# A Fourier mixer whose instructions are issued from one list of steps with a lead each

## Chip, core and metric

The kernel runs on one core of a Trainium2 chip. The metric is the device time in microseconds of one execution; lower is better. The core's engines run side by side: TensorE (PE; PEld are its weight loads), VectorE (DVE), ScalarE (ACT), GpSimd (POOL) and SyncE (SP, which only issues transfers here). Each engine takes its own instructions strictly in the order in which the program issued them.

## What is computed

A Fourier mixer, a dense squared-ReLU layer and a top-1 mixture of eight experts, on 8 sequences of 3072 tokens of width 256 (for the experts' sake the gate's part is left out here):

```python
def _attn_ref(x, w_r, w_i, b_r, b_i):
    X = np.fft.rfft(x, axis=1)
    Yr = Xr @ w_r - Xi @ w_i + b_r
    Yi = Xr @ w_i + Xi @ w_r + b_i
    Yr = np.sign(Yr) * np.maximum(np.abs(Yr) - 0.01, 0.0)
    Yi = np.sign(Yi) * np.maximum(np.abs(Yi) - 0.01, 0.0)
    return np.fft.irfft(Yr + 1j * Yi, n=3072, axis=1)
def _moe_ref(x, w_in, w_out):
    h = np.maximum(x @ w_in, 0.0)
    return (h * h) @ w_out
```

The weights `w_in` and `w_out` come in as 64-bit floats and are converted on the chip. Products are made to full single precision by splitting each operand into a high and a low part (tiles ending in `h` and `l`); `mm3` at L155 to L158 issues the three products high x high, high x low and low x high.

## The kernel before, in words

The Fourier transform of length 3072 is done as 48 x 64. The mixer's function `fft` has three streams of work.

`gen_a` (the x tiles, 64 of them, eight a sequence): load a tile of 96 x 1024 (L310), split it (xh and half of xl on VectorE, L317 and L318, the other half of xl on GpSimd, L319), six products with the constant `cc`, two copies out of PSUM on ScalarE (L336), one store to the DRAM scratch `ad` (L337).

`gen_b` (96 groups: 24 frequencies j for each of four pairs of sequences). Of a group: read bt from `ad`, two groups at a time (L354); load the tables tm (L360 for the first 24, which are also stored to `tmd` at L361, L363 for the others); split bt into bh and bl on VectorE (L375, L376); s2, three products, and the copy xe on ScalarE (L386); s3, four transposes (L393), then th from PSUM on ScalarE (L397), its negated half (L398), tl on VectorE (L399) and tl's negated half on ScalarE (L411); s4, 24 products with the mixing weights; y, the sum with the bias (L434) and t, its clamp (L435), on VectorE; y minus t on GpSimd (L436); the split into zh on ScalarE (L444) and zl on VectorE (L445); s5, three products, the copy gt on ScalarE (L457) and, every second group, the store to `gd` (L461).

`gen_w` converts `w_in` and `w_out` in 16 steps of eleven yields each; seven yields hold a VectorE operation, three a GpSimd operation, two a ScalarE operation.

The order is that of the generators. Before the loop 17 rounds of `gen_a` run, with the loads of the constants after the first, the mixing weights' loads in rounds 8 and 14 and two of `gen_w`'s loads in round 15. Then iteration t of `gen_b` issues, in this order for all engines: s3 of group t+1, s5 of t-2, s2 of t+2, the rest of s3, the reads and the split of t+3; then the x tile that is due (16 in 24 iterations), one yield of `gen_w`, the first half of s4 of t, another yield, zl and zh of t-1, the second half of s4, y, t and y minus t. There are eight PSUM banks in one ring, `ring()`, taken by s2, s3, s4, s5 and twice by an x tile. In the last two iterations the first tile of the next stage is read back (`c_load`, `c_split`) and transformed (`gen_c`).

After `fft`, `moe()` does the dense layer and the experts; the change does not touch it.

Of the kernel before, what the change touches and what calls it, by code (L numbers as in the profile page):

```python
# [122 lines left out]

def _step(gens, n=1):
    for _ in range(n):
        for g in gens:
            next(g, None)
# [8 lines left out]
def kernel(  # L136
# [15 lines left out]
    def f32(ap):  # L152
        return ap.bitcast(F32)
# [61 lines left out]
    def fft():  # L215
        with ExitStack() as es:
# [15 lines left out]

            def load_mix():
                raws = []
                for i, w in enumerate((w_r, w_i)):
                    raw = p2.tile([P, 2, 2, D], F32, tag="bt", name="raw", bufs=3)[:, 0]
                    SP.dma_start(out=raw, in_=w.rearrange("(c p) d -> p c d", p=P))
                    raws.append(raw)
                for v in range(2):
                    SP.dma_start(out=bias[0:64, v], in_=b_r.unsqueeze(0).to_broadcast([64, D]))  # L240
                    SP.dma_start(out=bias[64:128, v], in_=b_i.unsqueeze(0).to_broadcast([64, D]))
                SP.dma_start(out=bias[127:128, 1], in_=b_r.unsqueeze(0))
                yield
# [3 lines left out]
                yield  # L247
# [54 lines left out]
            def gen_a():  # L302
                NA = 8 * B
                xts, sp = {}, {}

                def load(i):
                    b, c = divmod(i, 8)
                    xt = pa2.tile([96, 4, D], F32, tag="xt", name="xt", bufs=3)
                    src = x[b].rearrange("(p t) d -> p (t d)", t=32)
                    SP.dma_start(out=xt.rearrange("p s d -> p (s d)"), in_=src[:, 4 * c * D:(4 * c + 4) * D])  # L310
                    xts[i] = xt

                def split(i):
                    xt = xts.pop(i).rearrange("p s d -> p (s d)")
                    xh = pa2.tile([96, 1024], F32R, tag="xh", name="xh")
                    xl = pa2.tile([96, 1024], F32R, tag="xl", name="xl")
                    V.tensor_copy(xh, xt)  # L317
                    V.tensor_sub(xl[:, :512], xt[:, :512], f32(xh[:, :512]))  # L318
                    G.tensor_sub(xl[:, 512:], xt[:, 512:], f32(xh[:, 512:]))  # L319
                    sp[i] = xh, xl  # L320

                for i in range(2):
                    load(i)
                for i in range(NA + 1):
                    if i + 2 < NA:
                        load(i + 2)
                    if i >= 1:
                        k = i - 1
                        b, c = divmod(k, 8)
                        xh, xl = sp.pop(k)  # L330
                        at = pa2.tile([96, 1024], F32, tag="at", name="at")
                        for q in range(2):
                            ps = ring()[:96]
                            sl = slice(q * 512, q * 512 + 512)
                            mm3(ps, cc[:, 0], cc[:, 1], xh[:, sl], xl[:, sl])
                            A.copy(at[:, sl], ps)  # L336
                        (A if k < 16 else SP).dma_start(  # L337
                            out=ad[b].rearrange("r (h t) d -> (r h) (t d)", h=2)[:, c * 1024:(c + 1) * 1024], in_=at)
                    if i < NA:
                        split(i)  # L340
                    yield

            NG = NJ * NP_

            def gen_b():
                bts, bs, xs, tt, ys, zs, gts, tms = {}, {}, {}, {}, {}, {}, {}, {}
                NJB = 2

                def load(jb):
                    pr, jb_ = divmod(jb, NJ // NJB)  # L350
                    bt = p2.tile([P, 2, NJB, D], F32, tag="bt", name="bt", bufs=3)
                    for bb in range(2):
                        src = ad[2 * pr + bb].rearrange("(j c) s d -> (c s) j d", c=2)
                        SP.dma_start(out=bt[:, bb], in_=src[:, jb_ * NJB:(jb_ + 1) * NJB, :])  # L354
                    bts[jb] = bt

                def load_t(j):
                    tm = p3.tile([P, 4, P], F32R, tag="tm", name="tm", bufs=7)
                    if j < NJ:
                        G.dma_start(out=tm, in_=c_tm[j])  # L360
                        SP.dma_start(out=tmd[j], in_=f32(tm))  # L361
                    else:
                        SP.dma_start(out=f32(tm), in_=tmd[j % NJ])  # L363
                    tms[j] = tm

                def s1(j):
                    jb, jj = divmod(j, NJB)
                    if jj == 0 and jb + 2 < NG // NJB:
                        load(jb + 2)
                    if j + 1 < NG:  # L370
                        load_t(j + 1)
                    src = bts[jb][:, :, jj, :]
                    bh = p2.tile([P, 2, D], F32R, tag="bh", name="bh")
                    bl = p2.tile([P, 2, D], F32R, tag="bl", name="bl")
                    V.tensor_copy(bh, src)  # L375
                    V.tensor_sub(bl, src, f32(bh))  # L376
                    bs[j] = bh, bl

                def s2(j):
                    bh, bl = bs.pop(j)  # L380
                    tm = tms[j]
                    ps = ring()
                    bh, bl = (a.rearrange("p b d -> p (b d)") for a in (bh, bl))
                    mm3(ps, tm[:, 0], tm[:, 1], bh, bl)
                    xe = p2.tile([P, 4, P], F32, tag="xe", name="xe")
                    A.copy(xe.rearrange("p a b -> p (a b)"), ps)  # L386
                    xs[j] = xe

                def s3(j):
                    xe = xs.pop(j)  # L390
                    ps = ring().rearrange("p (a q) -> p a q", a=4)
                    for a in range(4):
                        T.transpose(ps[:, a], xe[:, a], ident)  # L393
                    th = p2.tile([P, 4, 256], F32R, tag="th", name="th")
                    tl = p2.tile([P, 4, 256], F32R, tag="tl", name="tl")
                    if j % NJ:
                        A.copy(th[:, :, 64:192], ps)  # L397
                        A.activation(th[:, :, 0:64], ps[:, :, 64:128], AF.Copy, scale=-1.0)  # L398
                        V.tensor_sub(tl[:, :, 64:192], ps, f32(th[:, :, 64:192]))  # L399
                    else:  # L400
                        A.copy(th[:, :, 0:128], ps)
                        A.activation(th[:, :, 128:192], ps[:, :, 64:128], AF.Copy, scale=-1.0)
                        A.copy(th[:, :, 192:256], ps[:, :, 0:64])
                        V.tensor_sub(tl[:, :, 0:128], ps, f32(th[:, :, 0:128]))
                        V.tensor_copy(tl[:, :, 192:256], f32(tl[:, :, 0:64]))
                    tt[j] = th, tl

                def s3b(j):
                    th, tl = tt[j]
                    if j % NJ:  # L410
                        A.activation(tl[:, :, 0:64], f32(tl[:, :, 128:192]), AF.Copy, scale=-1.0)  # L411
                    else:
                        V.tensor_scalar(out=tl[:, :, 128:192], in0=f32(tl[:, :, 64:128]), scalar1=-1.0, scalar2=None, op0=ALU.mult)
                        for t in (th, tl):
                            for q in (191, 255):
                                V.tensor_scalar(out=t[:, :, q:q + 1], in0=ident[:, 0:4].unsqueeze(2), scalar1=0.0, scalar2=None, op0=ALU.mult)

                def s4(j):
                    th, tl = tt.pop(j)
                    o1, o2 = (64, 0) if j % NJ else (0, 128)  # L420
                    ps = ring()
                    for bb in range(2):
                        n = 0
                        for i, o in ((0, o1), (1, o2)):
                            for dc in range(2):
# [3 lines left out]
                        if bb == 0:  # L429
                            yield 1  # L430
# [584 lines left out]
```

## Time and profile before

| | us |
|---|---|
| median of three runs (4115.95 to 4117.76) | 4116.31 |
| the profiled execution | 4116.9 |
| its span, from first to last instruction | 4115.1 |
| of the span, TensorE busy | 3999.2 (97%) |
| VectorE busy | 3096.0 (75%) |
| ScalarE busy | 1970.1 (48%) |
| GpSimd busy | 987.5 (24%) |

A busy share is a sum over the span; the mixer takes about the first sixth of it, and the engines' shares there are others. TensorE's matmuls overlap, so that its busy time is not its peak. Two operations of VectorE back to back overlap by about 0.1 us: the start of one and the start of the next give its real cost, their durations a little more. An instruction that waits for a resource after it has started shows that wait as duration.

### The profile page before, as it was taken

To read this page: it belongs to the slowest core of one execution; us is meant where nothing else is said; L and a number is where in the kernel's file an instruction comes from. 1 tells how busy PE (TensorE), PEld (TensorE's weight loads), DVE (VectorE), ACT (ScalarE), POOL (GpSimd) and SP (SyncE) were. 2 spreads that over 40 slices of the span, in tenths; PEclk is the share of its full clock that TensorE was granted. 3 is DMA by queue.
4 is the path that set the end of the run, shared out by engine and by line. 5 is a ranking of instruction groups with operands and counts; after the bars stand their busy time and mean duration, and the time that the engine had idled before them with its cause. 6 is when DMAs were issued, how large, how long until landed. Compare 5 with 4: busy or idle time off the path is not lost. (4 is left out here: it accounts for less than half of the span.)

```text
span 4115.1 us, 72845 instructions
## 1 busy us (share of the span) xinstructions
PE 3999.2 (97%) x28092; PEld 3815.1 (93%) x28092; DVE 3096.0 (75%) x7513; ACT 1970.1 (48%) x3153; POOL 987.5 (24%) x715
## 2 busy tenths in 40 slices
PE   6888899999999999999999999999999999999998
PEld 4777788999999999999999999999999999999998
DVE  6999996788888888888888888888864545454465
ACT  3555555444444444444444444444443434343454
POOL 4655432111111111111111111111133222222232
PEclk7999999999999999999999999999999999999999
DMA  8876653000000000000000000000344444444373
GB/s 266 249 224 215 198 164 97 20 24 24 24 24 23 23 21 23 24 24 24 24 24 24 24 23 23 20 24 20 107 143 167 140 138 134 144 133 145 121 228 133
DMA packets 201779, 373.40 MB, mean 91 GB/s; under 512 B 18414, under 2 KB 128336, under 8 KB 201298
## 3 DMA queue, kind: packets, MB, share of 16 engines
q1 hardware_dynamic: 176578, 303.28, 23.5%
q0 software_dynamic: 23056, 59.11, 4.1%
q10 hardware_dynamic: 1792, 6.29, 0.5%
q8 instruction: 223, 3.65, 0.4%
q14 instruction: 130, 1.06, 0.1%
HBM read 259.08 MB, written 110.32 MB: 90 GB/s over the span
## 5 line engine op out<-in xcount | busy, mean ns | idle before, releaser
L783 PE MATMUL acc<-woh,gh 128*128 128x256 f32 x3072 | 882.1, 287 | 0.0
L763 ACT ACTIVATE rl<-g 128x768 f32<-128x768 f32 x512 | 415.6, 812 | 973.2 <-PE g L158 880.4
L156 PE MATMUL g<-xth,wih 128*128 128x384 f32 (+2 forms) x2512 | 858.4, 342 | 0.7 <-ACT gt L457 0.7
L784 PE MATMUL acc<-wol,gh 128*128 128x256 f32 x3072 | 857.6, 279 | 0.0
L157 PE MATMUL g<-xtl,wih 128*128 128x384 f32 (+2 forms) x2512 | 857.6, 341 | 0.0
L785 PE MATMUL acc<-woh,gl 128*128 128x256 f32 x3072 | 856.5, 279 | 0.0
L158 PE MATMUL g<-xth,wil 128*128 128x384 f32 (+2 forms) x2512 | 854.8, 340 | 0.0
L608 DVE CUSTOM_DVE_ANT_0 junk<-pay,wg 128x256 f32<-128x256 f32 x1536 | 651.0, 424 | 39.9
L770 DVE TENSOR_TENSOR gl<-sq,gh 128x768 fp32r<-128x768 f32 x512 | 612.6, 1197 | 32.4 <-DVE gh L769 1.4
L785 PEld LDWEIGHTS acc<-woh,gl 128*128 128x128 f32 x3072 | 581.1, 189 | 0.0
L783 PEld LDWEIGHTS acc<-woh,gh 128*128 128x128 f32 x3072 | 578.2, 188 | 0.0
L784 PEld LDWEIGHTS acc<-wol,gh 128*128 128x128 f32 x3072 | 578.1, 188 | 0.0
L872 DVE SCALAR_TENSOR_TENSOR hl<-g,hh 128x1024 fp32r<-128x1024 f32 x198 | 242.0, 1222 | 398.8 <-ACT hh L871 398.8
L553 POOL TENSOR_TENSOR hl<-ht,hh 96x1024 fp32r<-96x1024 f32 x64 | 153.9, 2405 | 1465.3 <-ACT hh L552 1465.3
L158 PEld LDWEIGHTS g<-xth,wil 128*128 128x128 f32 x2512 | 472.8, 188 | 13.3
L156 PEld LDWEIGHTS g<-xth,wih 128*128 128x128 f32 x2512 | 473.1, 188 | 11.8 <-ACT gt L457 1.2
L157 PEld LDWEIGHTS g<-xtl,wih 128*128 128x128 f32 x2512 | 473.3, 188 | 10.8
L871 ACT ACTIVATE hh<-g 128x1024 fp32r<-128x1024 f32 x198 | 203.4, 1027 | 543.3 <-PE g L158 529.4
L764 ACT ACTIVATE sq<-rl 128x768 f32<-128x768 f32 x512 | 434.2, 848 | 16.2
L901 POOL DMA_INDIRECT out_dram<-ot,ids x198 | 257.2, 1299 | 718.4 <-ACT ot L899 655.8
L769 DVE CAST gh<-sq 128x768 fp32r<-128x768 f32 x512 | 285.2, 557 | 76.5 <-ACT sq L764 73.2
L647 POOL DMA_INDIRECT bucket<-pay,pos x192 | 201.6, 1050 | 494.8 <-DMA bucket<-pay,pos 211.1
(192 smaller groups left out, 8339.1 us busy)
## 6 DMA issues: line engine op xcount, KB each, us to landing
r<-in_moe_w_dram SPq DMA_DIRECT2D x116, 1024.0 KB
xt<-in_x_dram SPq DMA_DIRECT2D x64, 384.0 KB
bt<-ad SPq DMA_DIRECT2D x96, 256.0 KB
gd<-gt SPq DMA_DIRECT2D x96, 256.0 KB
ht<-gd SPq DMA_DIRECT2D x64, 384.0 KB
xr<-bucket SPq DMA_DIRECT2D x41, 516.0 KB
ad<-at SPq DMA_DIRECT2D x48, 384.0 KB
tm<-tmd SPq DMA_DIRECT2D x72, 256.0 KB
```

The costliest lines, as they stand in the source:

```text
L156: T.matmul(ps, lhsT=lh, rhs=rh, start=first, stop=False)
L157: T.matmul(ps, lhsT=lh, rhs=rl, start=False, stop=False)
L158: T.matmul(ps, lhsT=ll, rhs=rh, start=False, stop=last)
L608: V.tensor_tensor_reduce(out=junk, in0=pay[:, g, 0:D], in1=wg[:, e], scale=1.0, scalar=0.0, op0=ALU.mult, op1=ALU.add, accum_out=lg[:, g, ...
L763: A.activation(r, ps[:, :, :TOK], AF.Relu)
L764: A.activation(g, r, AF.Square)
L769: V.tensor_copy(gh, g)
L770: V.tensor_sub(gl, g, f32(gh))
L783: T.matmul(o, lhsT=lh, rhs=woh[:, fc], start=st, stop=False, skip_group_check=True)
L784: T.matmul(o, lhsT=lh, rhs=wol[:, fc], start=False, stop=False, skip_group_check=True)
L785: T.matmul(o, lhsT=ll, rhs=woh[:, fc], start=False, stop=fc == 15, skip_group_check=True)
L901: ins = G.indirect_dma_start(out=out, out_offset=bass.IndirectOffsetOnAxis(ap=ids[:, g:g + 1], axis=0), in_=ot[:, g], in_offset=None, boun ...
```

## The change

The generators `gen_a` and `gen_b` are replaced by about thirty small functions, one for each step on one engine, and by a list, `MIX_ORDER`, of steps and leads: in iteration t, which runs from -8 to 97, the list is walked once, and a step with lead o issues its work for group t + o. For x tiles a table `a_it` says at which iterations t + o there is one (16 before each of the last three pairs of sequences). `W:1` is one yield of `gen_w`.

Other differences: bh is cast on ScalarE instead of VectorE. The high and low parts of t are one tile `th` of eight planes, and their negated halves are written by one ScalarE operation after `tl`. The store of the tables follows four iterations after their load. Before the loop 16 rounds of x tiles run (not 17, and no further tile is read ahead). All constants but `cc` and `ident` are loaded and set at iterations 56 and 66; the first weight step starts at iteration -2. The next stage's tile is read at iteration 90, split at 92, transformed from 93 on.

```diff
+MIX_ORDER = [(w.split(":")[0], int(w.split(":")[1])) for w in """
+    gt:-2 y:1 bl:5 tl:3 s5:-1 tms:2 A0:1 zh:0 gd:-2 W:1
+    A1:1 xh:2 t:1 neg:3 bh:6 bt:8 tm:6 s2:5 s4a:3 W:1
+    xlD:2 th:4 xt:4 xlP:2 xe:5 at0:1 s4b:3 s3:5 at1:1 zl:0
+    ymt:1 ad:0
+""".split()]
...
     def load_consts2():
-        SP.dma_start(out=ident, in_=c_ident)
         SP.dma_start(out=tri, in_=c_tri)
...
+
+    def init_consts():
         V.memset(ones, 1.0)
...
-            def gen_a():
...
-            def gen_b():
...
+            NA = 8 * B
             NG = NJ * NP_
+            NJB = 2
+            NPRE = 16
...
+            def a_high(i):
+                xhs[i] = pa2.tile([96, 1024], F32R, tag="xh", name="xh")
+                V.tensor_copy(xhs[i], xts[i])
+
+            def a_low(i):
+                xls[i] = pa2.tile([96, 1024], F32R, tag="xl", name="xl")
+                V.tensor_sub(xls[i][:, :512], xts[i][:, :512], f32(xhs[i][:, :512]))
+
+            def a_low_g(i):
+                xt = xts.pop(i)
+                G.tensor_sub(xls[i][:, 512:], xt[:, 512:], f32(xhs[i][:, 512:]))
...
+            def t_load(j):
+                tm = p3.tile([P, 4, P], F32R, tag="tm", name="tm", bufs=7)
+                if j < NJ:
+                    G.dma_start(out=tm, in_=c_tm[j])
+                else:
+                    SP.dma_start(out=f32(tm), in_=tmd[j % NJ])
+                tms[j] = tm
+
+            def t_store(j):
+                if j < NJ:
+                    SP.dma_start(out=tmd[j], in_=f32(tms[j]))
+
+            def b_high(j):
+                bhs[j] = p2.tile([P, 2, D], F32R, tag="bh", name="bh")
+                A.copy(bhs[j], bts[j // NJB][:, :, j % NJB, :])
+
+            def b_low(j):
+                bls[j] = p2.tile([P, 2, D], F32R, tag="bl", name="bl")
+                V.tensor_sub(bls[j], bts[j // NJB][:, :, j % NJB, :], f32(bhs[j]))
...
+            def t_high(j):
+                ths[j] = p2.tile([P, 8, 256], F32R, tag="th", name="th")
+                o = 64 if j % NJ else 0
+                A.copy(ths[j][:, 0:4, o:o + 128], tps[j])
+
+            def t_low(j):
+                thl, ps = ths[j], tps.pop(j)
+                o = 64 if j % NJ else 0
+                V.tensor_sub(thl[:, 4:8, o:o + 128], ps, f32(thl[:, 0:4, o:o + 128]))
+
+            def t_sign(j):
+                thl = ths[j]
+                if j % NJ:
+                    A.activation(thl[:, :, 0:64], f32(thl[:, :, 128:192]), AF.Copy, scale=-1.0)
+                else:
+                    A.activation(thl[:, :, 128:192], f32(thl[:, :, 64:128]), AF.Copy, scale=-1.0)
+                    A.copy(thl[:, :, 192:256], f32(thl[:, :, 0:64]))
+                    for q in (191, 255):
+                        A.activation(thl[:, :, q:q + 1], ident[:, 0:8].unsqueeze(2), AF.Copy, scale=0.0)
...
+            btok = {
+                "bt": b_load, "tm": t_load, "tms": t_store, "bh": b_high, "bl": b_low, "s2": s2_mm, "xe": s2_copy,
+                "s3": s3_mm, "th": t_high, "tl": t_low, "neg": t_sign, "s4a": lambda j: s4_mm(j, 0),
+                "s4b": lambda j: s4_mm(j, 1), "y": y_add, "t": y_clamp, "ymt": y_sub, "zh": z_high, "zl": z_low,
+                "s5": s5_mm, "gt": g_copy, "gd": g_store,
+            }
+            atok = {
+                "xt": a_load, "xh": a_high, "xlD": a_low, "xlP": a_low_g, "A0": lambda i: a_mm(i, 0),
+                "A1": lambda i: a_mm(i, 1), "at0": lambda i: a_copy(i, 0), "at1": lambda i: a_copy(i, 1),
+                "ad": lambda i: a_store(i, SP),
+            }
+            boff = [o for k, o in MIX_ORDER if k in btok]
+            aoff = dict((k, o) for k, o in MIX_ORDER if k in atok)
+            t0 = -max(boff)
+            lead = dict(MIX_ORDER)["bt"] - aoff["ad"] + 2
+            a_it, nxt = {}, t0 + max(aoff.values())
+            for pr in range(1, NP_):
+                end = NJ * pr - lead
+                for k in range(16):
+                    a_it[nxt + (end - nxt) * k // 15] = 16 * pr + k
+                nxt = end + 2
...
+            for i in range(NPRE + 1):
+                if i + 2 < NPRE:
+                    a_load(i + 2)
+                if i == NPRE - 2:
+                    load_mix()
...
+            split_mix()
 
             w = gen_w()
...
+            cg = None
+            for t in range(t0, NG - min(boff)):
+                if t == -2:
+                    next(w)
+                if t == NG - 40:
                     load_consts2()
+                if t == NG - 30:
+                    init_consts()
+                if t == NG - 6:
                     _drain(w)
                     ea.close()
                     open_shared()
                     c_load(0)
                     c_load(1)
+                if t == NG - 4:
+                    c_split(0)
+                if t == NG - 3:
                     cg = gen_c(0, ring)
+                for k, o in MIX_ORDER:
+                    j = t + o
+                    if k == "W":
+                        if t >= -2:
+                            _step([w], o if NP_ > 2 else 4)
+                    elif k in atok:
+                        if j in a_it:
+                            atok[k](a_it[j])
+                    elif 0 <= j < NG:
+                        btok[k](j)
+                if cg is not None:
                     next(cg, None)
             _drain(cg)
             c_split(1)
```

## Rows read from the trace of the kernel before

**Rows 1.** Busy by stretch: us, engines' busy us (times), PEclk, DMA share, GB/s.

```profile
0.00:88.00 88.00, 56.20 (x153) 31.11 (x154) 48.38 (x67) 30.30 (x56) 42.78 (x32) 0.75 0.87 260
88.00:505.00 417.00, 369.74 (x2369) 320.02 (x2368) 403.24 (x551) 235.38 (x480) 224.14 (x158) 0.99 0.72 225
505.00:638.00 133.00, 124.72 (x871) 113.27 (x870) 128.61 (x187) 77.40 (x161) 54.91 (x40) 1.00 0.52 165
...
687.00:4115.00 3428.00, 3407.08 (x24428) 3313.05 (x24427) 2485.56 (x6659) 1601.76 (x2405) 651.69 (x477) 1.00 0.21 67
```

**Rows 2.** The same stretches for L434 (y) alone; (x) counts the groups.

```profile
88.00:505.00 417.00, 42.38 (x62) 0.99 0.72 225
505.00:638.00 133.00, 17.80 (x26) 1.00 0.52 165
```

**Rows 3.** TensorE in order of time: start us, us, engine, line, operation.

```profile
342.11 0.40 PE L156 MATMUL r<-xh,cc 96*96 96x512 f32 x1
...
343.50 0.28 PE L156 MATMUL r<-wmh,th 128*128 128x256 f32 x1
...
655.53 0.60 PE L393 MATMUL r<-ident,xe 128*128 128x128 f32 x4
...
660.24 0.60 PE L393 MATMUL r<-ident,xe 128*128 128x128 f32 x4
```

**Rows 4.** VectorE in order of time, two periods, the second with an x tile.

```profile
348.09 0.68 DVE L434 TENSOR_TENSOR y<-r,bias 128x512 f32<-128x512 f32 x1
348.81 0.43 DVE L435 TENSOR_SCALAR t<-y 128x512 f32<-128x512 f32 x1
349.15 0.68 DVE L399 TENSOR_TENSOR tl<-r,th 128x512 fp32r<-128x512 f32 x1
349.75 1.21 DVE L375 CAST bh<-bt 128x512 fp32r<-128x512 f32 x1
351.00 0.69 DVE L376 TENSOR_TENSOR bl<-bt,bh 128x512 fp32r<-128x512 f32 x1
...
363.91 0.68 DVE L317 CAST xh<-xt 96x1024 fp32r<-96x1024 f32 x1
364.62 0.69 DVE L318 TENSOR_TENSOR xl<-xt,xh 96x512 fp32r<-96x512 f32 x1
365.23 1.77 DVE L445 TENSOR_TENSOR zl<-y,zh 128x512 fp32r<-128x512 f32 x1
```

**Rows 5.** GpSimd in order of time, the same stretch.

```profile
349.38 1.30 POOL L436 TENSOR_TENSOR y<-y,t 128x512 f32<-128x512 f32 x1 [2.81 <-DVE t L435]
...
357.60 2.68 POOL L319 TENSOR_TENSOR xl<-xt,xh 96x512 fp32r<-96x512 f32 x1 [1.75 <-issue]
...
364.72 1.73 POOL L319 TENSOR_TENSOR xl<-xt,xh 96x512 fp32r<-96x512 f32 x1 [1.75 <-issue]
```

**Rows 6.** Groups, 88 to 664 us: xcount, busy us, mean ns, idle before.

```profile
L375 DVE CAST bh<-bt 128x512 fp32r<-128x512 f32 x93 | 106.9, 1150 | 0.0
...
L319 POOL TENSOR_TENSOR xl<-xt,xh 96x512 fp32r<-96x512 f32 x42 | 83.2, 1981 | 66.6 <-issue 52.2 <-DVE xh L317 7.2 <-PE r L157 3.5
...
L444 ACT CAST zh<-y 128x512 fp32r<-128x512 f32 x93 | 57.5, 618 | 13.1 <-POOL y L436 12.0
```

**Rows 7.** The loop's start, in order of time on SP, VectorE, TensorE.

```profile
58.91 8.05 SPq L354 DMA_DIRECT2D bt<-ad  x4
...
68.43 0.43 DVE L375 CAST bh<-bt 128x512 fp32r<-128x512 f32 x1 [9.68 <-DMA bt<-ad]
...
87.61 0.28 PE L156 MATMUL r<-wmh,th 128*128 128x256 f32 x1
```

**Rows 8.** The loop's end, in order of time on VectorE, TensorE.

```profile
681.07 0.68 DVE L434 TENSOR_TENSOR y<-r,bias 128x512 f32<-128x512 f32 x1
...
686.53 0.69 PE L156 MATMUL g<-xth,wih 128*128 128x384 f32 x1 [0.67 <-ACT gt L457]
```

**Rows 9.** Waits of 88 to 664 us: who for whom, us, times, longest.

```profile
PE r L157 <- DVE zl L445: 53.4, 57, 2.8
```

More of the change, by code (lines that the diff above doesn't have):

```diff
@@ L300, in gen_w @@
                     yield
-            def gen_a():
[L303 to L341, printed above, removed]
@@ new lines, in fft, with a_load @@
+            NG = NJ * NP_
+            NJB = 2
+            NPRE = 16
+            xts, xhs, xls, ats, aps = {}, {}, {}, {}, {}
+            def a_load(i):
+                b, c = divmod(i, 8)
+                xt = pa2.tile([96, 4, D], F32, tag="xt", name="xt", bufs=3)
+                src = x[b].rearrange("(p t) d -> p (t d)", t=32)
+                SP.dma_start(out=xt.rearrange("p s d -> p (s d)"), in_=src[:, 4 * c * D:(4 * c + 4) * D])
+                xts[i] = xt.rearrange("p s d -> p (s d)")
@@ new lines, in a_copy, with a_store @@
+            def a_copy(i, q):
+                if q == 0:
+                    ats[i] = pa2.tile([96, 1024], F32, tag="at", name="at")
+                A.copy(ats[i][:, q * 512:q * 512 + 512], aps.pop((i, q)))
+            def a_store(i, eng):
+                b, c = divmod(i, 8)
+                eng.dma_start(out=ad[b].rearrange("r (h t) d -> (r h) (t d)", h=2)[:, c * 1024:(c + 1) * 1024],
+                              in_=ats.pop(i))
+            bts, bhs, bls, xs, xps, ths, tps, yps, ys, ts = {}, {}, {}, {}, {}, {}, {}, {}, {}, {}
@@ new lines, in fft, with b_load @@
+            zhs, zls, zps, gts, tms = {}, {}, {}, {}, {}
+            def b_load(j):
+                if j % NJB:
+                    return
+                pr, jb = divmod(j // NJB, NJ // NJB)
+                bt = p2.tile([P, 2, NJB, D], F32, tag="bt", name="bt", bufs=3)
+                for bb in range(2):
+                    src = ad[2 * pr + bb].rearrange("(j c) s d -> (c s) j d", c=2)
+                    SP.dma_start(out=bt[:, bb], in_=src[:, jb * NJB:(jb + 1) * NJB, :])
+                bts[j // NJB] = bt
@@ new lines, in b_low, with s2_mm, s2_copy @@
+            def b_low(j):
+                bls[j] = p2.tile([P, 2, D], F32R, tag="bl", name="bl")
+                V.tensor_sub(bls[j], bts[j // NJB][:, :, j % NJB, :], f32(bhs[j]))
+            def s2_mm(j):
+                xps[j] = ring()
+                bh, bl = (a.pop(j).rearrange("p b d -> p (b d)") for a in (bhs, bls))
+                mm3(xps[j], tms[j][:, 0], tms[j][:, 1], bh, bl)
+            def s2_copy(j):
+                xs[j] = p2.tile([P, 4, P], F32, tag="xe", name="xe")
+                A.copy(xs[j].rearrange("p a b -> p (a b)"), xps.pop(j))
@@ new lines, in s3_mm @@
+            def s3_mm(j):
+                tps[j] = ring().rearrange("p (a q) -> p a q", a=4)
+                xe = xs.pop(j)
+                for a in range(4):
+                    T.transpose(tps[j][:, a], xe[:, a], ident)
+            def t_high(j):
[6 more added lines that the diff above has]
+                V.tensor_sub(thl[:, 4:8, o:o + 128], ps, f32(thl[:, 0:4, o:o + 128]))
@@ new lines, in s4_mm @@
+            def s4_mm(j, bb):
+                thl = ths[j]
+                o1, o2 = (64, 0) if j % NJ else (0, 128)
+                if bb == 0:
+                    yps[j] = ring()
+                n = 0
+                for i, o in ((0, o1), (1, o2)):
+                    for dc in range(2):
+                        mm3(yps[j][:, bb * D:(bb + 1) * D], thl[:, 2 * bb + dc, o:o + P], thl[:, 4 + 2 * bb + dc, o:o + P],
+                            wmh[:, i, dc], wml[:, i, dc], first=n == 0, last=n == 3)
+                        n += 1
+                if bb:
+                    ths.pop(j)
@@ new lines, in y_add, with y_clamp, y_sub @@
+            def y_add(j):
+                ys[j] = p2.tile([P, 2, D], F32, tag="y", name="y")
+                bsel = bias[:, 0 if j % NJ else 1].unsqueeze(1).to_broadcast([P, 2, D])
+                V.tensor_add(ys[j], yps.pop(j).rearrange("p (b d) -> p b d", b=2), bsel)
+            def y_clamp(j):
+                ts[j] = p2.tile([P, 2, D], F32, tag="t", name="t")
+                V.tensor_scalar(out=ts[j], in0=ys[j], scalar1=-LAM, scalar2=LAM, op0=ALU.max, op1=ALU.min)
+            def y_sub(j):
+                G.tensor_sub(ys[j], ys[j], ts.pop(j))
@@ new lines, in g_copy, with g_store @@
+            def g_copy(j):
+                jb, jj = divmod(j, NJB)
+                if jj == 0:
+                    gts[jb] = p2.tile([P, 2, NJB, D], F32, tag="gt", name="gt")
+                A.copy(gts[jb][:, :, jj, :], zps.pop(j).rearrange("p (b d) -> p b d", b=2))
+            def g_store(j):
+                jb, jj = divmod(j, NJB)
+                if jj < NJB - 1:
+                    return
+                pr, jb_ = divmod(jb, NJ // NJB)
+                gt = gts.pop(jb)
+                for bb in range(2):
+                    SP.dma_start(
+                        out=gd[2 * pr + bb].rearrange("(j c) s d -> (c s) j d", c=2)[:, jb_ * NJB:(jb_ + 1) * NJB, :],
+                        in_=gt[:, bb])
@@ new lines, in fft @@
+            SP.dma_start(out=ident, in_=c_ident)
+            for i in range(2):
+                a_load(i)
+            for i in range(NPRE + 1):
[3 more added lines that the diff above has]
+                    load_mix()
+                if i >= 1:
+                    for q in range(2):
+                        a_mm(i - 1, q)
+                        a_copy(i - 1, q)
+                    a_store(i - 1, A)
+                if i < NPRE:
+                    a_high(i)
+                    a_low(i)
+                    a_low_g(i)
```

179 lines of the change are left out of this document (18 added, 161 removed).

## The prediction

> **What bounds the kernel now.** I read the stretches first: busy time of each engine from the start to the first mixing product (88 us), then by what runs beside the frequency loop [rows 1]. From 687 us on TensorE is busy in 3407 of 3428 us, and the change touches nothing there. What it can move lies in the first 687 us. In them VectorE, not TensorE, is full: 403 of 417 us while x tiles and weight steps run in the loop, 128.6 of 133 us when only weight steps remain, against TensorE's 370 and 125. The counts of y, one per group, turn this into periods [rows 2]: 62 groups in 417 us and 26 in 133 us, so 5.12 us a group without x tile. The 42 x tiles that the loop still has at 88 us [rows 6] all lie in the first stretch, so a period with one takes (417 - 20 x 5.12) / 42 = 7.5 us.
>
> TensorE alone needs less. Near the end of the loop, with neither x tile nor weight step, two transposes lie 4.71 us apart, without a pause; an x tile takes 1.39 us [rows 3]. So its floor is 4.7 us without and 6.1 us with an x tile.
>
> The reason why VectorE is full shows in single rows. Back to back it starts a two-input operation every 0.60 us (t_l to the next), t takes 0.34, and y followed by the t that reads it 0.72 [rows 4]. But the cast bh, which runs 0.43 us at 68.43 us with GpSimd idle [rows 7], runs 1.21 us when y-t is on GpSimd [rows 4, 5], and its mean is 1.15 us [rows 6]. zl runs 1.77 us behind GpSimd's part of an x tile and about 0.7 otherwise: VectorE and GpSimd take turns. GpSimd's x part took 1.73 us, 0.58 of that waiting for VectorE's own part, so it holds VectorE up for 1.15 us. It does not always come next: one took 2.68 us, when VectorE got further operations in first [rows 5]; with the mean of 1.98 [rows 6] about a third lose their turn. y and t_l have one input in PSUM and ran at 0.68 while GpSimd worked: they are the cover under which its work is free.
>
> The Trainium skill (SBUF — State Buffer, section Who interferes with whom) says that the two engines share a port pair, that an operation with two SBUF inputs or in a two-port mode takes it against GpSimd for the whole instruction, and that issue order decides who blocks. The rows agree (zl 1.77 against 0.7). It speaks against counting the moved cast's whole 1.15 us as won: a wait on the pair passes to whichever operation starts next.
>
> **The change part by part.** *VectorE's own time.* With an x tile a period before is y 0.72, t 0.34, t_l 0.60, bh 0.34, bl 0.60, xh 0.71 (xl reads it), xl 0.60, zl 0.60: 4.51 us. After, bh is on ScalarE and neither y nor xh is followed by its reader: y, bl, t_l, xl, zl at 0.60, xh 0.61, t 0.34: 3.95. The weight steps stay at two yields a group: eleven yields hold seven VectorE operations, two of 0.60 and five of 0.34, so 0.53 in both. Won: 0.56.
>
> *VectorE held up by GpSimd.* Before: the y part (1.30 us [rows 5]; held off by nobody, taken as 1.15 of hold like the x part) begins under t_l and holds bh for 0.9 (bl starts 1.25 after bh in place of 0.34: bh's 1.21 is the row); the x part holds the next one two times in three, 0.77. After: the x part is released by xh, and t, next on VectorE, slips in; then xl is held. The y part is queued behind the x part on GpSimd and comes up under xl, so that zl is next to be held. If GpSimd always gets its turn, 2 x 1.15 = 2.30; if it loses once, the y part ends under the next y and bl, 1.15 + 0.55 = 1.70; weighted with two thirds at each of two turns, 1.97. So 0.3 is given back: what was hidden under t_l no longer is. GpSimd's three weight operations in 5.5 groups hold about half of their 0.63 a group, 0.35, in both.
>
> *Sum of a period.* With x tile 4.51 + 0.53 + 1.67 + 0.35 = 7.06 before, measured 7.5; after 3.95 + 0.53 + 1.97 + 0.35 = 6.80. I take the difference, not the level: 7.5 - 0.26 = 7.24. Without x tile, before 3.20 + 0.53 + 0.9 + 0.35 = 4.98 (measured 5.12). After, 2.74 + 0.53, the y part 0.80 (a weight operation lies between t and zl in 7 of 11 cases, and GpSimd then holds zl; otherwise zl slips in and the y part ends under y and bl), and 0.35: 4.42. That is under TensorE's 4.7: TensorE becomes the bound there, 4.75 with some loss.
>
> *ScalarE.* It gains bh, 0.62 by its cast of the same size [rows 6]; the signs of t_h and t_l become one operation of the summed width in place of two. At most 0.62 more a group on an engine busy 235 of 417 us [rows 1]: hidden. The one added wait is that the sign operation now needs t_l; bh, t_h and x_e are queued behind it. TensorE issues s5, both x products and s2 ahead of the s4 that needs the signs, 2.8 us after its period begins, so I price it at nothing; without that cover it would cost the 0.62 in a group.
>
> *PSUM and SP.* y's bank is now held for two iterations, and with x tiles (six banks an iteration, eight in all) s5 of the second next one waits for y, which is first on VectorE: nothing while VectorE leads. On SP, storing the tables moves four iterations behind their loads, so the queue no longer waits for a load in flight; bt leads by two more groups. Nothing, or a gain, since DMA is at 0.72 [rows 1]; at the new mean period it would be 0.72 x 6.73 / 6.5 = 0.75, and more in the first 24 groups, which also read and store the tables.
>
> *Start.* SP held the first bt reads for 8 us, until all 16 tiles were stored, and bh followed at 68.4 [rows 7]. Up to there the DMA engines were 0.87 busy at 260 GB/s [rows 1]. Out of the way go three x loads of 384 KB, two weight loads of 512 KB and some 0.44 MB of constants and padding: 2.6 MB, at that rate 10 us. The x loads come back behind bt, but before s4 of group 0 only three x tiles are multiplied, not five. I take 12 us earlier for the first s4 (bounds 0, if store latency and not bandwidth sets the pace, and 18).
>
> *End.* From y of the last group to the first MoE product passed 5.5 us [rows 8]. The list carries both groups through at full pace but has the next stage's transform between them on every engine: 3 us more after the last y.
>
> *Total.* From the first s4 to the last y, before, 681.1 - 87.6 = 593.5 us. After: 45 periods with x tile x 7.24 = 326, less 4 for the first few, which have no y, t, zl yet; 44 x 4.75 = 209; 7 x 4.7 = 33: 564. So -29.5 in the loop, -12 at the start, +3 at the end: about -38. The profiled execution's span is 4115.1 us with 1.8 us around it (4116.9), 0.6 over the median of 4116.31. Forecast: 4116.3 - 38 = 4078.
>
> **The rivals.** (a) *TensorE takes over everywhere*: the longer leads, not VectorE's load, are what counted. For it: TensorE waits for zl, 53 us in 57 times [rows 9], the end of a chain through GpSimd, ScalarE and VectorE. Against it: what takes turns adds up to bl, zl, xl 1.80, t 0.34, xh 0.61, weights 0.53, GpSimd 2.30 + 0.63 = 6.2 us with x tile, over TensorE's 6.1, even if the rest is hidden entirely. 45 x 6.2 + 51 x 4.7 = 519: 74 less in the loop, 4116 - 74 - 12 + 3 = 4033. Half way there would be 4055. (b) *The waits only move*: GpSimd always gets its turn, and periods with x tile stay at 7.5 while those without reach 4.9; 338 - 4 + 51 x 4.9 = 584, and the start yields only 4: 4116 - 10 - 4 + 3 = 4105; with the start at 0 and no gain without x tile, 4115. (c) *Slower: GpSimd's two parts side by side hold VectorE, and ScalarE behind them*. If each of them costs its full 1.30 [rows 5], none of the weight work is hidden (0.63), and zh, second on ScalarE, waits for y-t so that signs and s4 follow late, a period with x tile comes to 3.95 + 0.53 + 2.60 + 0.63 + the 0.44 by which my sums fell short, 8.1 us. It decides from 7.6 us on: 45 x 8.1 + 51 x 5.0 - 4 = 615.5, 4116 + 22 - 4 + 3 = 4137. Against it: t_l and y cannot be held, so some cover always remains. (d) *The change doesn't do what it says* would mean that bh stays a charge of VectorE; the diff excludes it.
>
> **How the numbers follow.** Forecast, 4060 to 4100: 0.55. (a) and what lies towards it, below 4060: 0.17. (b), 4100 to 4120: 0.18. (c): 0.10. Leaving out the far half of (a) and of (c), the range is 4046 to 4116. Some 0.2% (8 us) is what a measurement can tell from no change. Faster by more than that, under 4108: forecast, (a) and a bit under half of (b), 0.78; within: 0.12; slower: 0.10.
>
> **What would show it.** After: bh on ScalarE at about 0.62; VectorE still about full with x tiles, with the long executions now at xl and zl and no longer at bh; periods near 7.2 with and 4.75 without x tile; first s4 near 76 us; MoE product near 648. Wrong at the turns if periods with x tile are at 6.2 (GpSimd under y and t_l) or near 8; wrong at the start if the first s4 comes after 84 us; wrong on ScalarE if t_h or x_e ends TensorE's waits.

## The result and the profile after

The changed kernel takes 4057.40 us (median of four runs, 4057.15 to 4060.97) against 4116.13 for the kernel before (four runs); the ratio is 0.9859, interval 0.9842 to 0.9876. It is faster by 58.7 us, where 38 were forecast, with 4046 to 4116 as the range. The profiled execution took 4057.15 us, its span is 4055.3.

Busy time by stretch, with the columns of [rows 1]; the stretches end at the first s4, at the last x tile, at the end of the weight steps (two short stretches left out) and at the end of the span:

```profile
0.00:82.00 82.00, 52.56 (x130) 28.76 (x131) 42.21 (x48) 27.20 (x51) 39.75 (x30) 0.69 0.84 236
82.00:470.00 388.00, 371.53 (x2436) 324.87 (x2435) 376.11 (x484) 259.99 (x496) 245.01 (x158) 1.00 0.81 250
470.00:580.00 110.00, 109.26 (x787) 102.72 (x787) 107.56 (x151) 82.38 (x154) 57.32 (x38) 1.00 0.59 186
...
627.50:4055.00 3427.50, 3406.64 (x24430) 3311.88 (x24428) 2487.65 (x6661) 1604.95 (x2408) 653.84 (x477) 1.00 0.21 67
```

The same for y alone, one per group, as [rows 2]:

```profile
82.00:470.00 388.00, 43.55 (x63) 1.00 0.81 250
470.00:580.00 110.00, 15.94 (x24) 1.00 0.59 186
```

63 groups with 44 x tiles now take 388 us where 62 with 42 took 417; TensorE is busy in 96% of them instead of 89%, and VectorE still in 97%. In the second stretch one of the 24 y lies only in part: 15.94 us at 0.68 each are 23.4 groups, and 110 / 23.4 = 4.70 us a group without x tile. TensorE is busy in 109.3 of the 110 us: there the bound has passed to TensorE, though VectorE, at 107.6, is still nearly full. With the other 19 groups of the first stretch at 4.70, a period with x tile comes to (388 - 19 x 4.70) / 44 = 6.79 us, by the way that gave 7.5 before. Counted straight from one y to the next on VectorE, the periods with x tile took 6.61 on average (7.19 before), and those without that lie among them 4.96 (5.68 before): the way by stretches puts what an x tile costs its neighbours on its own account.

The timeline of the changed kernel at the start and the end of the loop (SP's bt read, the first bh, the first x tile's product and the first s4; the last y, the first MoE product), as [rows 7, 8]:

```profile
44.94 16.15 SPq L362 DMA_DIRECT2D bt<-ad  x2
...
63.37 1.14 ACT L379 CAST bh<-bt 128x512 fp32r<-128x512 f32 x2 [4.17 <-DMA bt<-ad]
...
66.32 0.71 PE L164 MATMUL r<-xh,cc 96*96 96x512 f32 x1 [15.32 <-DVE xh L327]
...
82.34 0.28 PE L164 MATMUL r<-wmh,th 128*128 128x256 f32 x1
...
621.39 0.68 DVE L437 TENSOR_TENSOR y<-r,bias 128x512 f32<-128x512 f32 x1
...
627.46 0.65 PE L164 MATMUL g<-xth,wih 128*128 128x384 f32 x1
```

The first s4 begins at 82.3 us (before 87.6), the last y at 621.4 (681.1), the first MoE product at 627.5 (686.5). So the start brought 5.3 us, the loop from first s4 to last y 539.1 in place of 593.5, that is 54.4, and the end cost 0.6. After it nothing moved: TensorE is busy in 3406.6 us of the last stretch, 3407.1 before [rows 1].

Where VectorE is held now shows in its and GpSimd's timeline over one period with x tile:

```profile
361.24 0.42 DVE L441 TENSOR_SCALAR t<-y 128x512 f32<-128x512 f32 x1
...
361.45 2.30 POOL L335 TENSOR_TENSOR xl<-xt,xh 96x512 fp32r<-96x512 f32 x1 [4.82 <-DVE xh L327]
...
361.57 0.41 DVE L295 TENSOR_SCALAR wm<-wraw 128x512 uint32<-128x512 uint32 x1
...
361.91 0.68 DVE L331 TENSOR_TENSOR xl<-xt,xh 96x512 fp32r<-96x512 f32 x1
...
362.51 1.78 DVE L452 TENSOR_TENSOR zl<-y,zh 128x512 fp32r<-128x512 f32 x1
...
363.71 1.73 POOL L444 TENSOR_TENSOR y<-y,t 128x512 f32<-128x512 f32 x1
...
364.40 0.69 DVE L437 TENSOR_TENSOR y<-r,bias 128x512 f32<-128x512 f32 x1
...
365.01 0.99 DVE L383 TENSOR_TENSOR bl<-bt,bh 128x512 fp32r<-128x512 f32 x1
```

GpSimd's x part starts at 361.45, while VectorE runs t. Before GpSimd gets its turn VectorE has begun a weight operation and xl; then the x part runs and zl is held, 1.78 us in place of 0.68. The y part comes up at 363.71 under zl, runs mostly under the next y, and holds bl for the rest, 0.99 in place of 0.68.

Not every period goes like this. One period earlier the weight operation behind t was itself held, over both of GpSimd's parts:

```profile
354.01 1.36 POOL L335 TENSOR_TENSOR xl<-xt,xh 96x512 fp32r<-96x512 f32 x1 [2.22 <-issue]
...
354.14 2.78 DVE L291 TENSOR_SCALAR wm<-wraw 128x512 uint32<-128x512 uint32 x1
...
355.35 1.29 POOL L444 TENSOR_TENSOR y<-y,t 128x512 f32<-128x512 f32 x1
```

20 of the 44 x parts start under a t of some 0.41 us with a weight operation behind it. In 13 cases that operation and xl pass; in 7 it is held as here, 2.78 to 3.04 us. All 6 two-input weight operations (L293, L300) in that place are held, and 1 of the 14 with one input.

The means of the groups from 82 to 460 us, by line (columns of [rows 6]; L452 is zl, L383 bl, L441 t, L331 xl, L300 and L293 two-input steps of the weights, L379 the cast bh on ScalarE):

```profile
L452 DVE TENSOR_TENSOR zl<-y,zh 128x512 fp32r<-128x512 f32 x60 | 94.5, 1576 | 1.8 <-ACT zh L448 1.8
L383 DVE TENSOR_TENSOR bl<-bt,bh 128x512 fp32r<-128x512 f32 x61 | 60.1, 985 | 0.0
...
L441 DVE TENSOR_SCALAR t<-y 128x512 f32<-128x512 f32 x61 | 37.3, 611 | 0.0
...
L331 DVE TENSOR_TENSOR xl<-xt,xh 96x512 fp32r<-96x512 f32 x43 | 30.2, 703 | 0.0
L300 DVE TENSOR_TENSOR wu<-wu,wm 128x512 uint32<-128x512 uint32 x11 | 17.4, 1582 | 0.0
L293 DVE TENSOR_TENSOR wu<-wu,wm 128x512 uint32<-128x512 uint32 x12 | 12.8, 1070 | 0.0
...
L379 ACT CAST bh<-bt 128x512 fp32r<-128x512 f32 x62 | 37.8, 609 | 0.0
```

The wait that sat in bh (1.15 us, [rows 6]) now sits in zl, 1.58 on average; the weight steps are held as well, 1.58 and 1.07, where xl, not held, takes 0.70.

### The profile page after: what moved, and what is told of

Its sections match the earlier page's. It is cut to its first block, busy times and chain, and to the rows that moved or that the text cites. A ratio compares the mean times of both kernels' runs of the same rounds, so it can differ in the third digit from the quotient of the medians.

```text
span 4055.3 us, 72573 instructions
## 1 busy us (share of the span) xinstructions
PE 3985.2 (98%) x28092; PEld 3810.0 (94%) x28092; DVE 3047.6 (75%) x7393; ACT 2004.2 (49%) x3165; POOL 1015.1 (25%) x715
```

## The experiments

All times are medians; each verdict is against the runs of the kernel before that shared its chip. The medians of that kernel lie between 4114.7 and 4116.1 us, so a difference between two experiments is good to some 1.5 us at best. Loops and starts are read from one profiled execution each.

**The cast back on VectorE** (changed kernel, otherwise as it is).

```diff
             def b_high(j):
                 bhs[j] = p2.tile([P, 2, D], F32R, tag="bh", name="bh")
-                A.copy(bhs[j], bts[j // NJB][:, :, j % NJB, :])
+                V.tensor_copy(bhs[j], bts[j // NJB][:, :, j % NJB, :])
```

> The changed kernel with one step put back: bh is cast on VectorE again, at the same place of the list. If VectorE's load and its turns with GpSimd set the loop (theory), each of about 90 full periods gains 0.34 us of VectorE work and in the periods with x tile a further held operation of 0.3 to 0.5: 25 to 45 us slower than the changed kernel, 4082 to 4102. If the leads alone brought the gain (rival), moving one cast of 0.43 us back costs under 8 us: 4057 to 4065.

Measured: 4082.42 us, 0.9922 of before (0.9906 to 0.9939). That is 25 us over the changed kernel, at the near end of what the theory gave, and still 33 under the kernel before. So with the leads in place the cast's move is worth 25 us, and the list without it 33. For the loop my sum had counted of the list only the two pairs, y with t and xh with xl, that no longer follow each other. Its stretch with x tiles, as [rows 1]:

```profile
88.00:477.00 389.00, 362.89 (x2339) 314.24 (x2338) 382.39 (x533) 219.30 (x419) 266.31 (x156) 0.99 0.78 241
```

VectorE is as full as ever, 382 of 389 us: the order alone left the bound where it was. The stretch without x tile shows where the cast's move counts:

```profile
477.00:600.00 123.00, 118.22 (x820) 106.49 (x819) 120.66 (x179) 70.15 (x133) 55.57 (x37) 1.00 0.54 175
```

With 23 groups in it that is 5.35 us a group, no less than before (5.12), and 0.65 more than in the changed kernel. With x tiles the two run nearly alike, 62 groups and 43 tiles in 389 us against 63 and 44 in 388. So with the list in place the cast's move pays mostly in groups without x tile, not in those with one, where the expectation had it; and what the list brings without it lies with the x tiles and at the start (first s4 at 79.4 us, before 87.6). Which part of the list brings it, the leads or the order, wasn't tested.

**The cast alone** (kernel before, order and leads as they were).

```diff
-                    V.tensor_copy(bh, src)
+                    A.copy(bh, src)
                     V.tensor_sub(bl, src, f32(bh))
```

> The kernel before with one step of the change alone: bh is cast on ScalarE, order and leads as they were. Theory: VectorE loses 0.34 us of work and part of the 0.9 us for which GpSimd held bh (the rest passes to bl), so some 0.5 us in each of 88 full periods, 30 to 50 us faster than before, 4066 to 4086, if bl need not wait for ScalarE. Rival (the leads are what counts): bl now waits in its own iteration for a cast queued on ScalarE, and the gain is under 10 us: 4106 or more.

Measured: 4121.09 us against 4115.22, ratio 1.0012 (1.0003 to 1.0022): 5 to 6 us slower. The rival's reading holds. Its stretch with x tiles, as [rows 1]:

```profile
88.00:498.00 410.00, 360.50 (x2327) 311.99 (x2326) 327.01 (x479) 258.03 (x532) 220.84 (x155) 1.00 0.72 225
```

And the wait of VectorE for bh from 93 to 498 us (who for whom: us in total, times, longest):

```profile
DVE bl L376 <- ACT bh L375: 74.6, 59, 2.2
```

VectorE's busy time fell by 76 us against [rows 1], from 403 of 417 to 327 of 410, and none of it was won as time: bl waited 59 times for the cast that stood in ScalarE's queue in the same iteration, 1.26 us each time, about what the held cast had cost (1.15 on average, [rows 6]).

**The cast with a lead** (kernel before; the cast, and the read of its tile, one group ahead of bl).

```diff
+                bhs = {}
+
+                def s1h(j):
+                    jb, jj = divmod(j, NJB)
+                    if jj == 0 and jb + 2 < NG // NJB:
+                        load(jb + 2)
+                    bhs[j] = p2.tile([P, 2, D], F32R, tag="bh", name="bh")
+                    A.copy(bhs[j], bts[jb][:, :, jj, :])
...
                 def s1(j):
...
-                    bh = p2.tile([P, 2, D], F32R, tag="bh", name="bh")
+                    bh = bhs.pop(j)
...
-                    V.tensor_copy(bh, src)
                     V.tensor_sub(bl, src, f32(bh))
                     bs[j] = bh, bl
+                    if j + 1 < NG:
+                        s1h(j + 1)
...
+                s1h(0)
                 s1(0)
```

> The kernel before with bh cast on ScalarE, as in e2_before_bh_act, but one group earlier than bl, as the list does it. In e2 VectorE stood idle for 77 us of 410, 59 of its waits for this cast. If the missing lead is why e2 gained nothing (theory): VectorE's idle time goes back to some 10 us, and the loop gains what the moved work is worth, 0.3 to 0.7 us in 88 groups, 25 to 60 us faster than before, 4055 to 4090. If the wait of that cast only showed another wait behind it (rival): within 10 us of before, 4105 to 4125.

Measured: 4080.80 us, 0.9915 of before (0.9898 to 0.9931), 35 us faster. The stretch again:

```profile
88.00:480.00 392.00, 364.82 (x2380) 318.26 (x2379) 372.41 (x491) 264.06 (x547) 222.81 (x157) 1.00 0.76 240
```

VectorE is at 372 of 392 us, its waits for bh are gone. One step moved with one group of lead brings more than half of what the whole change brings; without the lead it brings nothing. The read of its tile went ahead with it, which wasn't tested apart; in the loop of the kernel before, VectorE shows no wait for that read.

**No x part on GpSimd** (changed kernel).

```diff
             def a_low(i):
...
-                V.tensor_sub(xls[i][:, :512], xts[i][:, :512], f32(xhs[i][:, :512]))
+                V.tensor_sub(xls[i], xts[i], f32(xhs[i]))
...
             def a_low_g(i):
-                xt = xts.pop(i)
-                G.tensor_sub(xls[i][:, 512:], xt[:, 512:], f32(xhs[i][:, 512:]))
+                xts.pop(i)
```

> The changed kernel with the whole low half of an x tile on VectorE, GpSimd's part gone. VectorE's own work grows by 0.53 us a tile, but nothing holds zl for 1.1 us. If the turns with GpSimd count as much as VectorE's work (theory): 0.57 us less in each of 44 periods with x tile, down to where TensorE's 6.1 us bounds them, 15 to 25 us faster than the changed kernel: 4032 to 4042. If VectorE's own work is what counts and the held time is idle time anyway (rival): 44 x 0.53 = 23 us slower, about 4080.

Measured: 4049.38 us, 0.9841 of before (0.9825 to 0.9857), 8 us under the changed kernel: the sign of the theory, a third to a half of its size. The timeline at the first s4 and the last y:

```profile
76.68 0.28 PE L164 MATMUL r<-wmh,th 128*128 128x256 f32 x1
...
610.70 0.68 DVE L436 TENSOR_TENSOR y<-r,bias 128x512 f32<-128x512 f32 x1
```

And zl and GpSimd's y part from 88 to 450 us, by line (L451, L443):

```profile
L451 DVE TENSOR_TENSOR zl<-y,zh 128x512 fp32r<-128x512 f32 x60 | 99.2, 1653 | 0.0
...
L443 POOL TENSOR_TENSOR y<-y,t 128x512 f32<-128x512 f32 x60 | 122.8, 2046 | 112.3 <-DVE t L440 89.5 <-ACT th L402 13.8 <-ACT th L412 4.5
```

The loop took 534.0 us, 5 less than the changed kernel's 539.1. zl is no less held than before, 1.65 us: with the x part gone, the y part takes its turn right there instead of under y. The 0.53 us a tile more on VectorE cost nothing net, so the rival (own work alone) falls. The first s4 came 5.7 us earlier than in the changed kernel, but with the changed kernel's x tiles it came at 79.4 us in the first experiment:

```profile
79.44 0.28 PE L164 MATMUL r<-wmh,th 128*128 128x256 f32 x1
```

So the start varies by some microseconds from run to run. The loop does too: it took 544.5 and 538.5 us in the next two experiments, whose edits lie at the start. The edit also takes GpSimd's part from the 16 x tiles before the loop. The 8 us are the edit's; how they divide between start and loop isn't shown.

**x tiles 16 to 18 read ahead of the first bt** (changed kernel).

```diff
-                if i + 2 < NPRE:
+                if i + 2 < NPRE + 3:
                     a_load(i + 2)
...
-                        if j in a_it:
+                        if j in a_it and not (k == "xt" and a_it[j] < NPRE + 3):
```

> The changed kernel with x tiles 16 to 18 read before the loop, ahead of the first bt read, so that SP's wait for the 16 stores no longer holds them back. If TensorE's idle time of 15 us at the start is that queue (theory), one or two x tiles are multiplied under the wait: 3 to 8 us faster than the changed kernel, 4049 to 4054. If the bytes set the pace (rival), the three loads delay the last stores by as much as they save: within 2 us.

Measured: 4055.57 us, 0.9852 (0.9836 to 0.9869), not to be told from the changed kernel. In its trace the first s4 starts at 77.2 us, 5.2 earlier than in the changed kernel's, but the last y at 621.65, so that the loop is 5.4 longer. By the time, TensorE's idle 15 us at the start were no loss that this edit could win back; why the loop took it back is open.

**Four buffers for the stores before the loop** (changed kernel).

```diff
                 if q == 0:
-                    ats[i] = pa2.tile([96, 1024], F32, tag="at", name="at")
+                    if i < NPRE and i % 2:
+                        ats[i] = p2.tile([P, 2, NJB, D], F32, tag="gt", name="gt")[:96].rearrange("p a b d -> p (a b d)")
+                    else:
+                        ats[i] = pa2.tile([96, 1024], F32, tag="at", name="at")
```

> The changed kernel with four buffers instead of two for the x tiles' results before the loop (every second one lies in the tile gt, unused until then). There ScalarE waits 1 to 2.6 us a tile for the store two tiles back. If that waiting sets the pace (theory A), the last of the 16 stores lands 5 to 10 us earlier: 4048 to 4053. If the transfers' bytes do (theory B), the stores only queue: within 2 us of 4057.

Measured: 4052.11 us, 0.9848 (0.9832 to 0.9864). The interval overlaps the changed kernel's, so the time alone doesn't decide; the trace shows what the buffers do. SP's first bt read, which waits for the last store:

```profile
43.83 12.13 SPq L365 DMA_DIRECT2D bt<-ad  x2
```

It is held until 55.96 us; the changed kernel's until 61.09, and in the four other traces with two buffers and no early x tiles until 59.6 to 60.4. So two buffers waiting for their stores, and not bytes alone, set when the last store landed. The first s4 comes at 77.6 us, which the spread of the other traces (76.7 to 82.3) covers, so how much of it reaches the loop isn't shown.

**t last, y and t_l over GpSimd's y part** (changed kernel, the list alone).

```diff
-    gt:-2 y:1 bl:5 tl:3 s5:-1 tms:2 A0:1 zh:0 gd:-2 W:1
-    A1:1 xh:2 t:1 neg:3 bh:6 bt:8 tm:6 s2:5 s4a:3 W:1
+    gt:-2 y:1 ymt:0 tl:3 bl:5 s5:-1 tms:2 A0:1 zh:0 gd:-2 W:1
+    A1:1 xh:2 neg:3 bh:6 bt:8 tm:6 s2:5 s4a:3 W:1
     xlD:2 th:4 xt:4 xlP:2 xe:5 at0:1 s4b:3 s3:5 at1:1 zl:0
-    ymt:1 ad:0
+    t:1 ad:0
```

> The changed kernel with t last in the list and GpSimd's y minus t released by it, and y and t_l next on VectorE: 1.2 us of operations with an input in PSUM over GpSimd's 1.15. Same instructions. If the turns of the two engines are what still fills VectorE (theory), zl and bl are no longer held by y minus t; with x tile 3.95 + 0.53 + 1.1 + 0.35 = 5.95 us, under TensorE's 6.1: TensorE becomes the bound, 10 to 20 us faster than the changed kernel, 4037 to 4047. If VectorE's own work or the chain to zl is the limit (rival), there is nothing to gain, and zh, released later, may cost: 4057 or more.

Measured: 4039.37 us, 0.9814 (0.9798 to 0.9831), 18 us under the changed kernel: the time that the theory gave, by a mechanism that it gave only in part. The same groups by line over the same 82 to 460 us as above:

```profile
L383 DVE TENSOR_TENSOR bl<-bt,bh 128x512 fp32r<-128x512 f32 x64 | 71.6, 1118 | 0.0
L452 DVE TENSOR_TENSOR zl<-y,zh 128x512 fp32r<-128x512 f32 x63 | 62.3, 988 | 2.0 <-ACT zh L448 1.4
L441 DVE TENSOR_SCALAR t<-y 128x512 f32<-128x512 f32 x64 | 61.2, 956 | 0.0
...
L331 DVE TENSOR_TENSOR xl<-xt,xh 96x512 fp32r<-96x512 f32 x44 | 41.5, 944 | 0.5
...
L293 DVE TENSOR_TENSOR wu<-wu,wm 128x512 uint32<-128x512 uint32 x12 | 8.2, 682 | 0.1
L300 DVE TENSOR_TENSOR wu<-wu,wm 128x512 uint32<-128x512 uint32 x12 | 8.2, 680 | 0.1
```

The instructions are the same, and the waits are fewer. zl with bl and t falls from 1.58 + 0.99 + 0.61 = 3.18 us a group to 0.99 + 1.12 + 0.96 = 3.07, 7 us over 64 groups. The two weight steps are no longer held, 0.68 each: 12 x (0.90 + 0.39) = 15 us. Against that xl, 0.94 for 0.70, gives 44 x 0.24 = 11 us back. That is a net 11 us of VectorE's time in this stretch. The wait left zl and the weight steps and went in part into bl, t and xl, where the theory had bl released too. The stretches with and without x tile:

```profile
82.00:460.00 378.00, 370.53 (x2475) 331.74 (x2474) 370.24 (x493) 261.90 (x507) 247.18 (x162) 1.00 0.83 258
460.00:570.00 110.00, 110.00 (x800) 103.97 (x799) 93.02 (x150) 81.01 (x154) 49.91 (x37) 1.00 0.60 191
```

With x tiles VectorE is still busy in 370 of 378 us; with 65 groups and 44 tiles in them, a period with x tile comes to (378 - 21 x 4.70) / 44 = 6.35 us, not yet TensorE's 6.1. Without x tile VectorE has 17 of 110 us to spare and the groups come no faster than in the changed kernel, 4.66 us from y to y on average against 4.65, which shows that TensorE bounds them there.

**Both** (the list of the last run, and no x part on GpSimd). To the list above it adds:

```diff
-                V.tensor_sub(xls[i][:, :512], xts[i][:, :512], f32(xhs[i][:, :512]))
+                V.tensor_sub(xls[i], xts[i], f32(xhs[i]))
...
-                G.tensor_sub(xls[i][:, 512:], xt[:, 512:], f32(xhs[i][:, 512:]))
```

> The order of the run before with, besides, the whole low half of an x tile on VectorE. In e3_x_dve GpSimd's y minus t took the turn that its x part had left, so that zl stayed held (1.15 us each time). Theory: with y minus t under y and t_l nothing of GpSimd's but the weight work is left to hold VectorE, 3.95 + 0.53 + 0.53 + 0.35 = 5.4 us with x tile; the loop goes by TensorE's 6.1 and 4.7 us, 20 to 28 us faster than the changed kernel, 4029 to 4037. Rival: if something else than these turns bounded e3_x_dve (TensorE, DMA at 0.81), 4045 to 4050 as there.

Measured: 4031.36 us, 0.9795 (0.9779 to 0.9811), 26 us under the changed kernel. The timeline at the first s4 and the last y:

```profile
78.90 0.28 PE L164 MATMUL r<-wmh,th 128*128 128x256 f32 x1
...
596.90 0.68 DVE L436 TENSOR_TENSOR y<-r,bias 128x512 f32<-128x512 f32 x1
```

The stretch with x tiles, as [rows 1]:

```profile
82.00:450.00 368.00, 363.82 (x2447) 327.02 (x2446) 337.60 (x492) 259.06 (x503) 144.92 (x116) 1.00 0.85 264
```

And VectorE's largest wait there:

```profile
DVE zl L451 <- ACT zh L447: 21.4, 22, 2.5
```

The loop takes 518.0 us. TensorE's floors give 45 x 6.1 + 51 x 4.7 = 514. Beside the x tiles VectorE has idle time of some size for the first time in a run of the changed kernel, 30 of 368 us, and TensorE is busy in 364 of 368, as the theory said. DMA, at 0.85, did not bound it either, as TensorE has no idle time left to give.

**All four edits together** (both of the last run, the early x tiles and the four buffers). To the last run it adds:

```diff
-                    ats[i] = pa2.tile([96, 1024], F32, tag="at", name="at")
+                    if i < NPRE and i % 2:
+                        ats[i] = p2.tile([P, 2, NJB, D], F32, tag="gt", name="gt")[:96].rearrange("p a b d -> p (a b d)")
+                    else:
+                        ats[i] = pa2.tile([96, 1024], F32, tag="at", name="at")
...
-                if i + 2 < NPRE:
+                if i + 2 < NPRE + 3:
...
-                        if j in a_it:
+                        if j in a_it and not (k == "xt" and a_it[j] < NPRE + 3):
```

> The edits of e8_cover_x_dve, e4_early_x and e5_four_at together. If the start's and the loop's gains are independent: the sum of the three, about 4024 to 4034; if the loop is bound by transfers once VectorE is free, no better than e8_cover_x_dve.

Measured: 4028.44 us, 0.9791 (0.9775 to 0.9807), 29 us under the changed kernel. It is the fastest of all, but its interval doesn't part it from the run before. In its trace the loop takes 517.6 us, as in that run, and the first s4 starts at 73.1, 5.8 earlier.

## Why the prediction was right, point by point

*What bounds the kernel.* Right: VectorE's load, GpSimd's turns included, not TensorE, and TensorE only where no x tile runs. The last experiments show it from the other side: the same instructions in another order win 18 us, and with most of the turns taken away VectorE has idle time and the loop lies within 1% of TensorE's floor.

*A period with x tile, 7.24 forecast, 6.79 measured.* This term was mis-sized, and it carries the difference: 45 x 0.45 = 20 us. I took the difference instead of the level, 7.5 - 0.26, and so carried the 0.44 by which my sum fell short of the kernel before over to the new one. The sum itself, 6.80, came out as measured, but in part by luck, since two of its parts were off in opposite directions. From y to y, 6.61 us, VectorE's operations ran 1.95 us longer than they do unheld, GpSimd's weight operations included, where 1.97 + 0.35 = 2.32 was priced. The rest, 4.66, was priced at 3.95 + 0.53 = 4.48: the next y starts 0.79 us behind zl when nothing is held (349.96 and 350.75 us), not 0.60. For the kernel before I priced bh at 0.34, though bl reads it; unheld, bl starts 0.46 behind the bh of 68.43 us:

```profile
68.89 0.69 DVE L376 TENSOR_TENSOR bl<-bt,bh 128x512 fp32r<-128x512 f32 x1
```

So moving bh away was worth 0.12 us a period more than I counted. And xl, which I expected to be held, is not (0.70); zl is, and the two-input weight steps are.

*A period without, 4.75 forecast, 4.70 measured.* TensorE took over as said.

*The parts taken as independent.* The forecast priced the cast's move and the list separately and gave the leads no worth of their own. The two runs on the kernel before show otherwise: the cast alone loses 5 us, with one group of lead it wins 35. My rival (a), that the leads count and not VectorE's load, was wrong as an alternative: a step moved off VectorE pays only if it also runs ahead. The list without the move wins 33 us as well, the two together 59.

*ScalarE.* Right: bh runs at 0.61 there, and ScalarE is busy in 260 of 388 us.

*The start, 12 forecast, 5.3 measured* (8.2 in the first experiment's trace and 5.8 with t last, whose x tiles before the loop are the same). I let bytes set the pace at 260 GB/s. The first bh came 5.1 us earlier (63.4 for 68.4), not 10; the buffers' run moved it by as much again (58.3). Then the x tiles stood in SP's queue behind the bt read that waits for the stores (from 44.9 to 61.1 us), which I had noted as a move and not priced; TensorE stood idle for 15.3 us until xh at 66.3. That this cost anything isn't shown: with the tiles read earlier nothing measurable was gained.

*The end, 3 us forecast, 0.6 measured.* The next stage's transform fits between the last groups.

*The rivals.* (b) and (c) had the x-tile period at 7.5 and 8.1; no row supports either. The measured 4057 lies under the 4060 to 4100 that I gave 0.55, in the band with 0.17, near the half-way point to (a), 4055. (a)'s reason is not what took it there: with all the leads and the cast on VectorE the kernel takes 4082.

## What to carry to other kernels

An operation that waits for a shared resource shows its wait as duration, and moving the operation away moves the wait to the next one; price the engine's whole period, with what each step can be covered by, and order the list so that operations that don't need the resource lie over the other engine's work. A step handed to another engine should run at least an iteration ahead of its reader: here its time otherwise returned as a wait of the same length. When a sum falls short of the measured period, ask what the rest is before carrying it over to the new one.

## What the runs showed of the hardware that was not expected

GpSimd and VectorE don't simply alternate. The x part that began under t at 361.45 let a weight operation and xl pass and took 2.30 us, where 1.15 is its own hold [rows 5]; the one that began under t at 354.01 held the weight operation behind t at once, and the y part followed under the same hold, 2.78 us in all. Of the 20 x parts that begin so, 13 went the first way and 7 the second, among these all 6 with a two-input weight operation next. The Trainium skill (SBUF — State Buffer, section Who interferes with whom) says that issue order decides who blocks. By the profile's start times the 7 agree; the 13 don't: GpSimd's part had started, and xl, with two inputs in SBUF and a later start, ran unheld. What decides between the two isn't shown.
